# A causal convolution's taps read from the transposition's PSUM bank, over whole rows, and a norm with both heads' reciprocals ahead of both products

## The chip, the core and the metric

The kernel runs on one core of a Trainium2 chip. The core has a matrix engine (PE, TensorE), three engines for elementwise work (DVE or VectorE, ACT or ScalarE, POOL or GpSimd), and SP, which here only issues DMA transfers. SBUF is the large on-chip memory. PSUM is the small memory that PE writes its results to. The metric is the time of one execution on the device in microseconds, the median of several runs.

## The reference, cut to what matters

```python
# attention: B=8, H=8, S=576, D=64
scores = (1/sqrt(D)) * q @ k.T                     # per batch and head
cum = cumsum(maximum(s, 0.0))
scores = where(causal, -1e9, scores + minimum(-(cum_i - cum_j), 0.0))
attn = exp(scores - max)
attn = attn / (sum(attn) + 1e-09)
x = attn @ v                                       # (B, S, 512) with the heads side by side
# gated linear unit with a causal convolution of 5 taps over S, per channel
gate_pre[:, t] = sum over k of conv_w[k] * x[:, t - 4 + k]
gate = 1 / (1 + exp(-gate_pre))
out = (gate * (x @ w_val)) @ w_out
```

## The kernel before

The work is cut into 32 passes n = 4b + p: a batch b (8 of them) and a pair of heads p (4 pairs), which makes 128 of the 512 channels of x. A pass goes through these steps:

- `scores` and `exps`: PE computes the scores of both heads in three steps into two double banks `s`, ACT takes the exponential of each step (L583) and writes the tile `P`.
- `av`: PE multiplies P with V, one head after the other, each into a PSUM bank of its own. Column 64 of each of the five row blocks is the row sum.
- `norm`: DVE takes the reciprocal of the row sums (L599) and multiplies (L600). The result goes to `xn` in SBUF. It is called once for each head.
- `x_T`: PE transposes the 128 channels of the pass into a bank as 128 channels by 576 positions, in bf16.
- `x_evac`: DVE copies the bank (L611) into `xT` in SBUF, behind four columns of zeros.
- `tap`: five taps of the convolution. The row of 576 is done in two halves of 288. The first tap of a half writes the product of x and one weight per channel (L623 on ACT or L625 on DVE) into a PSUM bank `gs`. Each of the other four (L629, on DVE) reads xT shifted by one column, multiplies and adds the sum. Three of them write back to the bank and the last one writes the tile `gp` in SBUF. The table `ON_ACT` gives the first taps of 21 of the 32 passes to ACT.
- `tanh`: ACT turns gp into `th` (L633).
- `val` and `glu`: when all four passes of a batch are in xT, PE multiplies x with w_val (L653), in two halves for each pass, and DVE multiplies each half with the gate (L659).
- `outp`, `out_evac`, `store`: PE multiplies with w_out (L665), ACT copies to SBUF (L670), SP stores.

Eight PSUM banks exist. Four of them are the two double banks of the scores. The other four, named m0 to m3, are shared by all else: the transpositions of q and k (`qk_T`, copied by ACT at L533), the two heads of av, x, gs, val and out. Of gp there are two buffers, so that a tap that writes gp first waits for the tanh of the pass two before.

The order is not written by hand. Each step is a task with an engine, an assumed duration, the tasks it depends on, the buffers it takes and gives back, and a due time, which is the pass number plus an offset from the table `DUE`. The class `Plan` plays the tasks through once before the program is built: every engine takes the ready task with the earliest due time. The instructions are then emitted in that order, and each engine works through its own list strictly in that order. At run time an instruction waits for the instructions that it depends on, also on its own engine.

The weights of the convolution come transposed as `cwT` (L478). The scaled w_val is `wv` (L455). Both stand on DVE ahead of the first tap. On SP the load of w_val (L453) stands behind the loads of the first two batches of q and k.

Of the kernel before, what the change touches and what calls it, by code (L numbers as in the profile page):

```python
# [16 lines left out]
B, H, S, D = 8, 8, 576, 64  # L17
DM = 512
NKB = 5
# [184 lines left out]
def pcol(kb, qb):  # L204
    if kb == qb:
        return kb * 128
    if qb == 4:
# [13 lines left out]

DUE = dict(av=0.35, norm=0.78, xt=0.86, xe=-3.88, tap=1.56, dtap=0.01, tanh=0.36, cpe=-12.17, val=4.61,
           dval=0.23, out=9.61, dout=0.77, oute=-13.36, qt=-3.41, qe=-3.11, tt=-2.05, te=-14.54, s4=-1.53,
           vp=-12.15, cast=-20.65, lqk=-9.83, lv=17.78)

ON_PE = ()
PE_CHUNK = 2

ON_ACT = tuple(n for n in range(32) if n % 3)


class Plan:
# [115 lines left out]
def main_path(ctx, tc, q, k, v, s, moe_w_val, moe_conv_w, moe_w_out, out, okcnt):  # L350
# [5 lines left out]
    nc = tc.nc  # L356
# [125 lines left out]
    T = {}  # L482
# [110 lines left out]
                nc.tensor.matmul(ps[:, qb * 65:qb * 65 + 65], lhsT, Vps[b % 2][:, kb, 2 * p + hh, :],  # L593
                                 start=(kb == 0), stop=(kb == qb))

    def norm(n, hh):
        b, p = divmod(n, 4)
        pv = slot["av", n, hh].rearrange("t (g d) -> t g d", d=65)
        nc.vector.reciprocal(recs[:, n, hh], pv[:, :, 64])  # L599
        nc.vector.tensor_tensor(xns[b % 2][:, :, p * 128 + hh * 64:p * 128 + hh * 64 + 64], pv[:, :, 0:64],  # L600
                                recs[:, n, hh].unsqueeze(2).to_broadcast([128, NKB, 64]), ALU.mult)

    def x_T(n):
        b, p = divmod(n, 4)
        pt = slot["x", n] = bank(("x", n), [128, S], BF16)
        for i in (4, 0, 1, 2, 3):
            nc.tensor.transpose(pt[:, WIN[i]:WIN[i] + 128], xns[b % 2][:, i, p * 128:(p + 1) * 128], ident)  # L607

# [1 line left out]
        b, p = divmod(n, 4)  # L610
        nc.vector.tensor_copy(xTs[b % 2][:, p, 4:4 + S], slot["x", n])  # L611

    def tap(n, hf, m):

        b, c = divmod(n, 4)
        o = hf * 288
        xc = xTs[b % 2][:, c, o:o + 292]
        if m == 0:
            slot["gs", n, hf] = bank(("gs", n, hf), [128, 288])
            if hf == 0:  # L620
                slot["g", n] = work("gp", n, [128, S], FP32)
            if n in ON_ACT:
                nc.scalar.activation(out=slot["gs", n, hf], in_=xc[:, 4:292], func=AF.Copy, scale=cwT[:, c, 4:5])  # L623
            else:
                nc.vector.tensor_scalar(slot["gs", n, hf], xc[:, 4:292], cwT[:, c, 4:5], None, ALU.mult)  # L625
        else:
            gs = slot["gs", n, hf]
            dst = slot["g", n][:, o:o + 288] if m == 4 else gs
            nc.vector.scalar_tensor_tensor(dst, xc[:, m - 1:m + 287], cwT[:, c, m - 1:m], gs, ALU.mult, ALU.add)  # L629

    def tanh(n):
        th = slot["t", n] = work("th", n, [128, S], FP32)
# [42 lines left out]
    for b in range(B):  # L675
# [58 lines left out]
        for p in range(4):  # L734
            n = n0 + p
            es = []
            for i in range(3):
                take = [("s", ("s", n, i))] + ([("P", n)] if i == 0 else [])
                t = T["s", n, i] = add("PE", (0.56, 0.27, 0.27)[i], n + 0.3 * i, lambda n=n, i=i: scores(n, i),
                                       [T["qe", b, p], t_te, T.get(("s", n, i - 1)), T.get(("s", n - 1, 2))],  # L740
                                       take=take, mode="R")
                es.append(add("ACT", 0.905, n + 0.3 * i, lambda n=n, i=i: exps(n, i), [t],
                              give=[("s", ("s", n, i))]))
            ns = []
            for hh in range(2):
# [3 lines left out]
                ns.append(add("DVE", 0.62, n + DUE["norm"] + 0.1 * hh, lambda n=n, hh=hh: norm(n, hh),  # L749
                              [t, T.get(("xt", n - 8))], give=[("m", ("av", n, hh))]))  # L750
            T["norm", n] = ns[1]
            t = T["xt", n] = add("PE", 0.3, n + DUE["xt"], lambda n=n: x_T(n), ns, take=[("m", ("x", n))], mode="N")

            T["xe", n] = add("DVE", 0.37, n + DUE["xe"], lambda n=n: x_evac(n),
                             [t] + [T.get(("val", n0 - 8 + c, hf)) for c in range(4) for hf in range(2)]
                             + T.get(("conv", n - 8), []), give=[("m", ("x", n))])
            ths = []
            if PE_CONV(b, p):
                cs = []
                for hf in range(2):  # L760
                    t = add("PE", 1.85, n + DUE["cpe"], lambda n=n, hf=hf: conv_pe(n, hf), [T["xe", n], t_dg] + cs[-1:],
                            take=[("m", ("g", n, hf))], mode="N")
                    cs.append(t)
                    ths.append(add("ACT", 0.42, n + DUE["cpe"] + 0.2, lambda n=n, hf=hf: tanh_pe(n, hf), [t] + ths,
                                   take=[("th", n)] if hf == 0 else [], give=[("m", ("g", n, hf))]))
                T["conv", n] = cs
            else:
                ends = []
                for hf in range(2):
                    t = ends[0] if hf else None  # L770
                    for m in range(5):
                        take = [("gp", n)] if m + hf == 0 else []
                        if m == 0:
                            take = take + [("m", ("gs", n, hf))]
                        t = add("ACT" if m == 0 and n in ON_ACT else "DVE", 0.37, n + DUE["tap"] + (hf * 2.5 + m * 0.5) * DUE["dtap"],
                                lambda n=n, hf=hf, m=m: tap(n, hf, m), [T["xe", n], t_cw, t], take=take,
                                give=[("m", ("gs", n, hf))] if m == 4 else [])
                    ends.append(t)
                T["conv", n] = ends
# [102 lines left out]
```

## Time and profile before

| | |
|---|---|
| time, median of 3 runs | 270.92 us (270.29 to 271.18) |
| time of the profiled execution | 271.83 us |
| its span | 270.0 us |
| mean granted TensorE clock | 0.938 |
| taps on DVE (L625, L629) | 278 instructions, 143.8 us |
| first taps on ACT (L623) | 42 instructions, 21.1 us |
| norm on DVE, whole run (L599, L600) | 64 + 64 instructions, 12.0 + 31.5 us |
| copies of x on DVE (L611) | 32 instructions, 14.5 us |

The span runs from the first to the last instruction of the program. The rest of an execution's time lies around it. A row of the profile for a group of instructions gives the line, the engine, the operation, the tiles written and read, the shapes and the count, then the busy time and the mean duration in ns, and then the idle time of the engine just before these instructions with what ended it. A row of waits says who waited for whom, with the sum in us, the number of times and the longest one.

### The profile page before, as it was taken

The numbers are of one execution on the slowest core, as the hardware profiler recorded it, in microseconds if no ns is written. First come the engines' busy times: TensorE is split into PE (matmuls) and PEld (weight loads), VectorE is DVE, ScalarE is ACT, GpSimd is POOL, SyncE is SP. The second block draws the span as 40 slices with busy tenths as digits, with TensorE's granted clock in tenths as the row PEclk, the third lists the DMA queues.
The fourth block names the chain that finished last, engine by engine and source line by source line (L and its number), as shares of the span: only waits on it lengthen the run. The fifth ranks groups of instructions, "written<-read, shape, count | busy, mean of one in ns | idle before, by whom it ended". The sixth has DMA issues, their size and how long they took to land. (4 is left out here: it accounts for less than half of the span.)

```text
span 270.0 us, 6360 instructions
## 1 busy us (share of the span) xinstructions
PE 197.8 (73%) x2539; PEld 127.8 (47%) x2561; DVE 226.0 (84%) x524; ACT 194.9 (72%) x267; POOL 73.3 (27%) x73
## 2 busy tenths in 40 slices
PE   0788776766598679876849886887878776986660
PEld 0465642554456445553436553555445544543420
DVE  4453699899999898999987998999899999999920
ACT  2789788434888989878865787977987797684330
POOL 9204236457022810300930057042033000000000
PEclk9999965688889999999967999999999999999998
DMA  6999999989259970794421910752560120043133
GB/s 168 258 297 304 179 264 300 195 230 328 62 187 227 311 233 23 165 261 142 162 71 26 224 68 2 168 107 80 122 114 37 53 89 2 2 155 136 42 104 105
DMA packets 69232, 40.50 MB, mean 150 GB/s; under 512 B 47109, under 2 KB 63493, under 8 KB 69194
## 3 DMA queue, kind: packets, MB, share of 16 engines
q1 hardware_dynamic: 69194, 40.01, 56.7%
q8 instruction: 22, 0.36, 0.6%
q14 instruction: 16, 0.13, 0.2%
HBM read 30.57 MB, written 9.44 MB: 148 GB/s over the span
## 5 line engine op out<-in xcount | busy, mean ns | idle before, releaser
L583 ACT ACTIVATE P<-s 128x1024 bf16<-128x1024 f32 x96 | 95.1, 1027 | 14.4 <-PE s L580 9.5
L629 DVE SCALAR_TENSOR_TENSOR m<-xT,cwT,m 128x288 f32<-128x288 bf16 x192 | 99.6, 521 | 6.3 <-ACT m L623 1.6
L653 PE MATMUL m<-xT,wv 128*128 128x288 bf16 x256 | 43.6, 309 | 10.1 <-DVE gp L629 8.5
L538 PE MATMUL s<-QKT 64*128 64x128 bf16 (+4 forms) x576 | 41.4, 253 | 13.0 <-ACT P L583 10.6
L593 PE MATMUL m<-Vp,P 128*128 128x65 bf16 x960 | 40.8, 199 | 10.1 <-DVE gp L629 7.4
L500 POOL TENSOR_TENSOR Vp<-vst,w 128x650 bf16<-128x650 f32 x28 | 35.1, 1283 | 42.2 <-DMA vst<-in_v_dram 36.7
L665 PE MATMUL m<-wo,glu 128*128 128x512 bf16 x138 | 39.5, 384 | 9.5 <-DVE gp L629 7.3
L593 PEld LDWEIGHTS <-P 128*128 128x128 bf16 x960 | 36.4, 101 | 19.2 <-DVE gp L629 8.0
L538 PEld LDWEIGHTS <-QKT 64*128 64x128 bf16 x576 | 21.6, 99 | 34.0 <-issue 26.3
L533 ACT COPY QKT<-m 128x1024 bf16<-128x1024 bf16 x32 | 32.2, 1017 | 6.5 <-PE m L529 6.3
L653 PEld LDWEIGHTS <-wv 128*128 128x128 bf16 x256 | 24.6, 103 | 23.3 <-issue 13.6
L629 DVE SCALAR_TENSOR_TENSOR gp<-xT,cwT,m 128x288 f32<-128x288 bf16 x64 | 32.8, 514 | 2.1
L633 ACT ACTIVATE th<-gp 128x576 f32<-128x576 f32 x32 | 21.9, 684 | 15.9 <-DVE gp L629 15.6
L600 DVE TENSOR_TENSOR xn<-m,recs 128x320 bf16<-128x320 f32 x64 | 31.5, 492 | 2.2
L623 ACT ACTIVATE m<-xT,cwT 128x288 f32<-128x288 bf16 x42 | 21.1, 506 | 15.9 <-DVE glu L659 5.8
L670 ACT COPY ot<-m 128x512 f32<-128x512 f32 (+1 forms) x40 | 23.3, 584 | 11.9 <-PE m L665 9.4
L659 DVE SCALAR_TENSOR_TENSOR glu<-th,m 128x288 bf16<-128x288 f32 x64 | 26.7, 448 | 1.8 <-PE m L653 1.5
L665 PEld LDWEIGHTS <-glu 128*128 128x128 bf16 x160 | 14.4, 98 | 22.8 <-issue 7.5
L490 POOL CAST qb<-qkf 128x2048 bf16<-128x2048 f32 x7 | 13.3, 1894 | 37.1 <-issue 22.4
L529 PE MATMUL m<-ident,qb 128*128 128x128 bf16 x128 | 13.1, 227 | 12.0 <-DVE chalf L432 6.4
L607 PE MATMUL m<-ident,xn 128*128 128x128 bf16 x160 | 14.8, 225 | 6.4 <-DVE xn L600 5.1
L611 DVE COPY xT<-m 128x576 bf16<-128x576 bf16 x32 | 14.5, 452 | 4.4 <-PE m L607 4.3
(59 smaller groups left out, 160.2 us busy)
## 6 DMA issues: line engine op xcount, KB each, us to landing
out_dram<-ot SPq DMA_DIRECT2D x32, 256.0 KB, 2.1
qkf<-in_q_dram SPq DMA_DIRECT2D x7, 1024.0 KB, 5.9
qkf<-in_k_dram SPq DMA_DIRECT2D x7, 1024.0 KB, 7.9
vst<-in_v_dram SPq DMA_DIRECT2D x28, 256.0 KB, 5.0
vst<-in_v_dram SPq DMA_DIRECT2D x15, 128.0 KB, 4.3
first<-in_q_dram SPq DMA_DIRECT2D x4, 256.0 KB, 3.5
first<-in_k_dram SPq DMA_DIRECT2D x4, 256.0 KB, 3.6
tail<-in_q_dram SPq DMA_DIRECT2D x8, 128.0 KB, 8.8
```

The lines of the kernel that those rows point to most:

```text
L500: eng.tensor_tensor(Vps[b % 2][:, :, h], vst[:, :, h], w[:, :, b * 8 + 2 * p:b * 8 + 2 * p + 2].unsqueeze(3).to_broadcast([128, NKB, 2, 65 ...
L533: nc.scalar.copy(QKTs[b % 2][:, :, p, 0:512].rearrange("d w (x j) -> d w x j", j=4), slot["qt", b, p].rearrange("d w (j x) -> d w x j", j=4))
L538: nc.tensor.matmul(ps[:, hh, c0:c0 + nq], QKTs[b % 2][r, 1, p, k0:k0 + 128], QKTs[b % 2][r, 0, p, q0:q0 + nq], **kw)
L583: nc.scalar.activation(out=slot["Pt", n][:, :, step * 512:(step + 1) * 512], in_=slot["s", n, step], func=AF.Exp, scale=0.125)
L593: nc.tensor.matmul(ps[:, qb * 65:qb * 65 + 65], lhsT, Vps[b % 2][:, kb, 2 * p + hh, :], start=(kb == 0), stop=(kb == qb))
L600: nc.vector.tensor_tensor(xns[b % 2][:, :, p * 128 + hh * 64:p * 128 + hh * 64 + 64], pv[:, :, 0:64], recs[:, n, hh].unsqueeze(2).to_broad ...
L629: nc.vector.scalar_tensor_tensor(dst, xc[:, m - 1:m + 287], cwT[:, c, m - 1:m], gs, ALU.mult, ALU.add)
L633: nc.scalar.activation(out=th, in_=slot["g", n], func=AF.Tanh, scale=0.5)
L653: nc.tensor.matmul(ps, wv[:, dc, c * 128:(c + 1) * 128], xTs[b % 2][:, dc, 4 + o:4 + o + 288], start=(dc == 0), stop=(dc == 3))
L659: nc.vector.scalar_tensor_tensor(glus[b % 2][:, c, o], slot["t", n][:, o], 1.0, slot["v", n, hf], ALU.add, ALU.mult)
L665: nc.tensor.matmul(ps, glus[b % 2][:, c, WIN[i]:WIN[i] + 128], wo[:, c, :], start=(c == 0), stop=(c == 3))
L670: nc.scalar.copy(ot[r, :], slot["o", b, i][r, :])
```

## The change

Each pass loses the two banks gs. The taps read the bank of x itself, not the copy in SBUF, and run over the whole row in one piece. The sum is kept in gp in SBUF from the first tap on, which is a product alone, written with the newest weight over all 576 columns. The other four add x times an older weight, shifted to the right by `sh` = 4, 3, 2 and 1 columns, over the columns from sh on, so the zeros ahead of xT aren't needed by the taps. The bank of x is given back by the fifth tap and no longer by the copy. The copy stays, since val reads it. All first taps go to DVE. A norm is one task for both heads: two reciprocals and then two products. It starts when both heads' av are done, and gives both banks back at its end. The transposition of x also takes a gp buffer, in the plan. The table of due times is another one, which moves tasks on all engines.

```diff
-DUE = dict(av=0.35, norm=0.78, xt=0.86, xe=-3.88, tap=1.56, dtap=0.01, tanh=0.36, cpe=-12.17, val=4.61,
...
+DUE = dict(av=0.31, norm=0.64, xt=1.09, xe=0.37, tap=1.88, dtap=0.55, tanh=0.13, cpe=-12.44, val=4.58,
...
-ON_ACT = tuple(n for n in range(32) if n % 3)
+ON_ACT = ()
...
-    def norm(n, hh):
+    def norm(n):
         b, p = divmod(n, 4)
...
+        pvs = [slot["av", n, hh].rearrange("t (g d) -> t g d", d=65) for hh in range(2)]
+        for hh in range(2):
+            nc.vector.reciprocal(recs[:, n, hh], pvs[hh][:, :, 64])
+        for hh in range(2):
+            nc.vector.tensor_tensor(xns[b % 2][:, :, p * 128 + hh * 64:p * 128 + hh * 64 + 64], pvs[hh][:, :, 0:64],
+                                    recs[:, n, hh].unsqueeze(2).to_broadcast([128, NKB, 64]), ALU.mult)
...
-    def tap(n, hf, m):
+    def tap(n, m):
...
+        x, gp = slot["x", n], slot["g", n]
+        sh = (4 - (m - 1)) % 5 if m else 0
         if m == 0:
...
-                nc.vector.tensor_scalar(slot["gs", n, hf], xc[:, 4:292], cwT[:, c, 4:5], None, ALU.mult)
+                nc.vector.tensor_scalar(gp, x, cwT[:, c, 4:5], None, ALU.mult)
         else:
-            gs = slot["gs", n, hf]
-            dst = slot["g", n][:, o:o + 288] if m == 4 else gs
-            nc.vector.scalar_tensor_tensor(dst, xc[:, m - 1:m + 287], cwT[:, c, m - 1:m], gs, ALU.mult, ALU.add)
+            nc.vector.scalar_tensor_tensor(gp[:, sh:S], x[:, 0:S - sh], cwT[:, c, 4 - sh:5 - sh], gp[:, sh:S],
+                                           ALU.mult, ALU.add)
...
-                             + T.get(("conv", n - 8), []), give=[("m", ("x", n))])
+                             + T.get(("conv", n - 8), []), give=[("m", ("x", n))] if on_pe else [])
...
+                t = T["xe", n]
+                for m in range(5):
+                    act = m == 0 and n in ON_ACT
+                    t = add("ACT" if act else "DVE", 0.54 if act else 0.67, n + DUE["tap"] + m * DUE["dtap"],
+                            lambda n=n, m=m: tap(n, m), [t_cw, t], give=[("m", ("x", n))] if m == 4 else [])
```

How the order moves is seen at three places. In the rows the number right behind a name is the buffer (m0 to m3 are the four shared banks), and the number behind the underscore tells one use of it from another. In the kernel after the change the reciprocal stands at L600, the product at L602, the copy at L615, the first tap at L626 and the others at L628; the lines of before are those named above.

The first place is DVE in pass 21, in the second half of the run. Before, with the sum in the bank m3:

```order
L625 TENSOR_SCALAR m3_3005<-xT1_119,cwT_130 128x288
L629 SCALAR_TENSOR_TENSOR m3_3005<-xT1_119,cwT_130,m3_3005 128x288 x3
L629 SCALAR_TENSOR_TENSOR gp1_3006<-xT1_119,cwT_130,m3_3005 128x288
L599 RECIPROCAL recs_126<-m0_3008 128x5
L600 TENSOR_TENSOR xn1_117<-m0_3008,recs_126 128x5x64
L625 TENSOR_SCALAR m3_3064<-xT1_119,cwT_130 128x288
L629 SCALAR_TENSOR_TENSOR m3_3064<-xT1_119,cwT_130,m3_3064 128x288 x2
L611 COPY xT1_119<-m2_3073 128x576
L629 SCALAR_TENSOR_TENSOR m3_3064<-xT1_119,cwT_130,m3_3064 128x288
L629 SCALAR_TENSOR_TENSOR gp1_3006<-xT1_119,cwT_130,m3_3064 128x288
L599 RECIPROCAL recs_126<-m0_3082 128x5
L600 TENSOR_TENSOR xn1_117<-m0_3082,recs_126 128x5x64
```

Behind the first of these rows the sum of the first half is finished in gp1, then comes a norm of one head, and then the second half. After, with x in the bank m1 and the sum in gp1:

```order
L615 COPY xT1_119<-m1_2824 128x576
L626 TENSOR_SCALAR gp1_2825<-m1_2824,cwT_130 128x576
L628 SCALAR_TENSOR_TENSOR gp1_2825<-m1_2824,cwT_130,gp1_2825 128x572
L628 SCALAR_TENSOR_TENSOR gp1_2825<-m1_2824,cwT_130,gp1_2825 128x573
L600 RECIPROCAL recs_126<-m2_2833 128x5
L600 RECIPROCAL recs_126<-m3_2859 128x5
L602 TENSOR_TENSOR xn1_117<-m2_2833,recs_126 128x5x64
L602 TENSOR_TENSOR xn1_117<-m3_2859,recs_126 128x5x64
L628 SCALAR_TENSOR_TENSOR gp1_2825<-m1_2824,cwT_130,gp1_2825 128x574
L628 SCALAR_TENSOR_TENSOR gp1_2825<-m1_2824,cwT_130,gp1_2825 128x575
```

Before, the ten taps of the pass stand in two runs of five with a norm of one head between and one behind them, and the second run has the copy of the next pass in it. After, the copy is followed at once by the first tap of the same pass, five taps stand in the place of ten, and the norm of the next pass stands as four instructions between the third tap and the fourth.

The second place is ACT at about the same time, in passes 22 and 23. Before:

```order
L623 ACTIVATE m0_3160<-xT1_119,cwT_130 128x288
L583 ACTIVATE P0_3047<-s0_3128 128x2x512
L670 COPY ot0_3182<-m3_3152 128x512
L623 ACTIVATE m2_3197<-xT1_119,cwT_130 128x288
L533 COPY QKT1_113<-m1_3171 128x2x512
L558 ACTIVATE P40_100<-s0_3185 128x8x64
L583 ACTIVATE P1_3137<-s1_3136 128x2x512
L670 COPY ot1_3236<-m0_3213 64x512
L623 ACTIVATE m3_3254<-xT1_119,cwT_130 128x288
L623 ACTIVATE m0_3273<-xT1_119,cwT_130 128x288
L583 ACTIVATE P1_3137<-s0_3230 128x2x512
L583 ACTIVATE P1_3137<-s1_3277 128x2x512
```

Four of these twelve rows are first taps (L623). After, from the tanh of pass 21 to that of pass 22 and one row on:

```order
L633 ACTIVATE th3_2971<-gp1_2825 128x576
L583 ACTIVATE P0_2878<-s1_2966 128x2x512
L583 ACTIVATE P1_2976<-s0_2975 128x2x512
L533 COPY QKT0_112<-m3_2995 128x2x512
L583 ACTIVATE P1_2976<-s1_3005 128x2x512
L670 COPY ot0_3055<-m0_3012 128x512
L558 ACTIVATE P40_100<-s0_3029 128x8x64
L533 COPY QKT1_113<-m3_3045 128x2x512
L633 ACTIVATE th4_3077<-gp0_2916 128x576
L670 COPY ot1_3095<-m0_3065 64x512
```

The first taps between the exponentials, copies and tanhs are gone from ACT's list, and nothing stands in their place.

The third place is DVE at the first taps of the run. Before, from the third copy on:

```order
L611 COPY xT0_118<-m2_513 128x576
L599 RECIPROCAL recs_126<-m1_519 128x5
L600 TENSOR_TENSOR xn0_116<-m1_519,recs_126 128x5x64
L599 RECIPROCAL recs_126<-m3_536 128x5
L600 TENSOR_TENSOR xn0_116<-m3_536,recs_126 128x5x64
L611 COPY xT0_118<-m1_605 128x576
L455 TENSOR_SCALAR wv_127<-qkf2_175 128x2048
L478 COPY cwT_130<-m2_633 128x20
L625 TENSOR_SCALAR m1_640<-xT0_118,cwT_130 128x288
L629 SCALAR_TENSOR_TENSOR m1_640<-xT0_118,cwT_130,m1_640 128x288 x3
L629 SCALAR_TENSOR_TENSOR gp0_641<-xT0_118,cwT_130,m1_640 128x288
L625 TENSOR_SCALAR m0_673<-xT0_118,cwT_130 128x288
```

Here four norms and four copies stand ahead of wv, cwT and the first tap. After, from the scaling of wv on:

```order
L455 TENSOR_SCALAR wv_127<-qkf2_175 128x2048
L478 COPY cwT_130<-m2_557 128x20
L626 TENSOR_SCALAR gp0_351<-m0_350,cwT_130 128x576
L628 SCALAR_TENSOR_TENSOR gp0_351<-m0_350,cwT_130,gp0_351 128x572
L626 TENSOR_SCALAR gp1_441<-m3_440,cwT_130 128x576
L628 SCALAR_TENSOR_TENSOR gp0_351<-m0_350,cwT_130,gp0_351 128x573
L628 SCALAR_TENSOR_TENSOR gp1_441<-m3_440,cwT_130,gp1_441 128x572
L628 SCALAR_TENSOR_TENSOR gp0_351<-m0_350,cwT_130,gp0_351 128x574
L600 RECIPROCAL recs_126<-m1_515 128x5
L600 RECIPROCAL recs_126<-m2_609 128x5
L602 TENSOR_TENSOR xn0_116<-m1_515,recs_126 128x5x64
L602 TENSOR_TENSOR xn0_116<-m2_609,recs_126 128x5x64
```

Ahead of these rows stand three norms and two copies, so that wv, cwT and the first tap have moved ahead of one norm and two copies. The taps of passes 0 and 1 alternate, out of the banks m0 and m3, and the norm of the fourth pass stands between them.

More of the change, by code (lines that the diff above doesn't have):

```diff
@@ L605, in x_T @@
         pt = slot["x", n] = bank(("x", n), [128, S], BF16)
+        if not PE_CONV(b, p):
+            slot["g", n] = work("gp", n, [128, S], FP32)
         for i in (4, 0, 1, 2, 3):
@@ L748, in main_path @@
                                         give=[("P", n)] if hh else [], mode="N")
[L749 to L752, printed above, removed]
+            ns = [add("DVE", 1.1, n + DUE["norm"], lambda n=n: norm(n), [t, T.get(("xt", n - 8))],
+                      give=[("m", ("av", n, hh)) for hh in range(2)])]
+            T["norm", n] = ns[0]
+            on_pe = PE_CONV(b, p)
+            t = T["xt", n] = add("PE", 0.3, n + DUE["xt"], lambda n=n: x_T(n), ns,
+                                 take=[("m", ("x", n))] + ([] if on_pe else [("gp", n)]), mode="N")
             T["xe", n] = add("DVE", 0.37, n + DUE["xe"], lambda n=n: x_evac(n),
                              [t] + [T.get(("val", n0 - 8 + c, hf)) for c in range(4) for hf in range(2)]
[L756 removed]
+                             + T.get(("conv", n - 8), []), give=[("m", ("x", n))] if on_pe else [])
             ths = []
@@ L767, in main_path @@
             else:
[L768 to L779, printed above, removed]
+                t = T["xe", n]
[3 more added lines that the diff above has]
+                            lambda n=n, m=m: tap(n, m), [t_cw, t], give=[("m", ("x", n))] if m == 4 else [])
+                T["conv", n] = [t]
                 ths = [add("ACT", 0.59, n + DUE["tanh"], lambda n=n: tanh(n), [t], take=[("th", n)], give=[("gp", n)])]
```

15 lines of the change are left out of this document (3 added, 12 removed).

## The prediction

> **What bounds the kernel now.** I read the page first for the busy shares, then the span cut into three stretches, then what VectorE (DVE) waits for, and last the starts of neighbouring DVE instructions.
>
> ```profile
> PE 197.8 (73%) x2539; PEld 127.8 (47%) x2561; DVE 226.0 (84%) x524; ACT 194.9 (72%) x267; POOL 73.3 (27%) x73
> ...
> 0.00:33.70 33.70, 21.91 (x333) 16.24 (x334) 16.86 (x37) 24.66 (x33) 13.00 (x28) 1.00 0.96 241
> 33.70:258.40 224.70, 171.91 (x2189) 110.01 (x2211) 209.16 (x487) 167.35 (x231) 60.34 (x45) 0.93 0.53 138
> 258.40:270.00 11.60, 3.94 (x19) 1.57 (x16) 0.00 (x0) 2.92 (x5) 0.00 (x0) 0.89 0.32 110
> ```
>
> The cuts are the first tap (33.7 us) and the last glu product (258.4 us). In each row the length comes first, then PE, PEld, DVE, ACT and POOL. Between the cuts DVE is busy 209.16 of 224.70 us, so 15.5 us are left. Few of them are waits for another engine:
>
> ```profile
> DVE xT L611 <- PE m L607: 1.6, 2, 1.2
> DVE m L629 <- ACT m L623: 1.6, 3, 0.6
> DVE glu L659 <- PE m L653: 1.5, 4, 0.5
> DVE recs L599 <- PE m L593: 0.7, 2, 0.4
> ```
>
> These are 5.4 us; the rest is the hand-over from one DVE instruction to the next. So in this stretch the time is DVE's: its list of work, one after the other. Before it DVE is half idle (DMA share 0.96), behind it DVE does nothing. What DVE does there:
>
> ```profile
> L629 DVE SCALAR_TENSOR_TENSOR m<-xT,cwT,m 128x288 f32<-128x288 bf16 x192 | 99.6, 521 | 6.3 <-ACT m L623 1.6
> L629 DVE SCALAR_TENSOR_TENSOR gp<-xT,cwT,m 128x288 f32<-128x288 bf16 x64 | 32.8, 514 | 2.1
> L600 DVE TENSOR_TENSOR xn<-m,recs 128x320 bf16<-128x320 f32 x56 | 27.5, 492 | 1.9
> L659 DVE SCALAR_TENSOR_TENSOR glu<-th,m 128x288 bf16<-128x288 f32 x64 | 26.7, 448 | 1.8 <-PE m L653 1.5
> L611 DVE COPY xT<-m 128x576 bf16<-128x576 bf16 x28 | 12.6, 452 | 1.7 <-PE m L607 1.6
> L625 DVE TENSOR_SCALAR m<-xT,cwT 128x288 f32<-128x288 bf16 x22 | 11.4, 517 | 0.6
> L599 DVE RECIPROCAL recs<-m 128x5 f32<-128x5 f32 x56 | 10.4, 187 | 1.0 <-PE m L593 0.7
> ```
>
> The taps (L629 and L625, 278 instructions) are 143.8 us of it. What one instruction really takes of the list is the distance between starts:
>
> ```profile
> 149.92 0.18 DVE L599 RECIPROCAL recs<-m 128x5 f32<-128x5 f32 x1
> 150.14 0.49 DVE L600 TENSOR_TENSOR xn<-m,recs 128x320 bf16<-128x320 f32 x1
> 150.55 1.63 DVE L629 SCALAR_TENSOR_TENSOR m<-xT,cwT,m 128x288 f32<-128x288 bf16 x3
> 152.08 0.45 DVE L611 COPY xT<-m 128x576 bf16<-128x576 bf16 x1
> 152.45 0.50 DVE L629 SCALAR_TENSOR_TENSOR gp<-xT,cwT,m 128x288 f32<-128x288 bf16 x1
> 152.88 0.18 DVE L599 RECIPROCAL recs<-m 128x5 f32<-128x5 f32 x1
> ...
> 162.91 0.45 DVE L611 COPY xT<-m 128x576 bf16<-128x576 bf16 x1
> 163.47 0.52 DVE L625 TENSOR_SCALAR m<-xT,cwT 128x288 f32<-128x288 bf16 x1
> ...
> 173.64 1.17 DVE L659 SCALAR_TENSOR_TENSOR glu<-th,m 128x288 bf16<-128x288 f32 x3
> ```
>
> A tap whose result the next instruction reads takes (1.63 − 0.52)/2 = 0.555 us: its duration and 0.035 of hand-over. A tap with a stranger behind it takes 152.88 − 152.45 = 0.43: the stranger starts 0.09 before the tap ends. Likewise reciprocal 0.22 with its product behind it, product 0.41, copy 0.37 (0.56 where the next tap reads what it copied), glu (1.17 − 0.45)/2 = 0.36.
>
> In the order of before, 191 of the 278 taps stand ahead of an instruction that reads their result and 87 do not; 20 copies stand ahead of a reader, 8 do not. So the list is 191 × 0.555 + 87 × 0.43 = 143.4; 28 passes × 2 × 0.63 = 35.3 of norms; 20 × 0.56 + 8 × 0.37 = 14.2 of copies; 64 × 0.36 = 23.0 of glus; 2.5 for the scaling of wo and the check of the reciprocals: 218.4. With 5.4 of waits it is 223.8 of the 224.7 measured. The method misses 0.9 us, which I carry along.
>
> **Taps, part one: their number and length.** The ten half-row taps of a pass become five of 572 to 576 columns; all five are on DVE. No row shows this instruction. Its length follows from two others:
>
> ```profile
> L500 DVE TENSOR_TENSOR Vp<-vst,w 128x650 bf16<-128x650 f32 x4 | 3.3, 833 | 4.1 <-DMA vst<-in_v_dram 2.9 <-ACT w L445 1.2
> ...
> L811 DVE SCALAR_TENSOR_TENSOR ok<-recs,ok 128x320 f32<-128x320 f32 x1 | 0.5, 492 | 0.0
> ```
>
> 330 more columns cost 341 ns, 1.033 ns each. A tap of 288 columns takes 521 ns, so 576 take 0.521 + 288 × 0.00103 = 0.82 us. Ends: the glu row, which also reads PSUM and SBUF and writes SBUF, gives 0.448 + 0.298 = 0.75; two half taps without any saving give 1.04. I take 0.82, the same operation with the same per-partition factor. The first tap (a product alone) has as near relatives L625, 0.517 + 0.298 = 0.815, and the copy L611, 0.452 for the whole row, since that moves bf16 to bf16; its output is now f32 as L625's is, so 0.82 too.
>
> [...]
>
> **Part two: who stands behind a tap.** In the new order only 60 of 160 taps are followed by the next tap of their own chain; 100 have a stranger behind them. Taps: 60 × (0.82 + 0.035) + 100 × (0.82 − 0.09) = 51.3 + 73.0 = 124.3, against 143.4.
>
> **Norms and copies.** Two reciprocals stand together, and the first product needs only the first of them, so the pair hides in the 0.22 that one took: 0.22 + 2 × 0.41 = 1.04 per pass instead of 1.26. One pass more than before falls behind the first tap: 29 × 1.04 = 30.2. The first tap reads the PSUM bank, no longer the copy, so every copy takes 0.37: 30 × 0.37 = 11.1 (two more than before). Glus 23.0 and the 2.5 stay. New list: 124.3 + 30.2 + 11.1 + 23.0 + 2.5 = 191.1, which is 27.3 less.
>
> **Start and end of the stretch.** The first tap still needs the scaled wv and cwT ahead of it:
>
> ```profile
> 19.78 1.26 SPq L453 DMA_DIRECT2D qkf<-in_moe_w_val_dram  x1
> ...
> qkf<-in_moe_w_val_dram SPq DMA_DIRECT2D x1, 1024.0 KB, 11.1
> ...
> 31.93 1.65 DVE L455 TENSOR_SCALAR wv<-qkf 128x2048 bf16<-128x2048 f32 x1
> 33.50 0.16 DVE L478 COPY cwT<-m 128x20 f32<-128x20 f32 x1
> 33.77 0.52 DVE L625 TENSOR_SCALAR m<-xT,cwT 128x288 f32<-128x288 bf16 x1
> ```
>
> wv lands at 19.78 + 11.1 = 30.9. SP's order is the same up to there, and the row that made DVE late (the fourth copy) now stands behind, so the first tap comes at 30.9 + 1.84 = 32.7. The tail of 11.6 us keeps its work: tanh, val, glu, out, copy and store of the last pass.
>
> **ScalarE, POOL, SP.** ScalarE loses 42 first taps, and with them DVE's 1.6 us of waits for it:
>
> ```profile
> L623 ACT ACTIVATE m<-xT,cwT 128x288 f32<-128x288 bf16 x42 | 21.1, 506 | 15.9 <-DVE glu L659 5.8 <-DVE xT L611 4.7 <-DVE gp L629 2.6
> ```
>
> They are off the path (ACT is busy 167.35 of 224.70), so the 21.1 us are worth only those 1.6; I leave them in the waits, as new ones will take their place. POOL's casts and products and SP's loads move by a few places; no DVE wait names either, so I price this at nothing. Their cover is POOL's 164 idle us in the stretch.
>
> **New waits.** A bank of x is now held from its transposition through all five taps: 0.37 + 4 × 0.73 + 0.855 with a norm of 1.04 between, about 5.2 us. Before, it was 0.8 for x and two sums of 5 × 0.555, 6.4 us. The first head's bank is held some 0.5 longer. So the four banks carry about as much, in a shorter time. What DVE can now outrun is PE:
>
> ```profile
> 103.70 2.33 PE L653 MATMUL m<-xT,wv 128*128 128x288 bf16 x16
> ...
> 151.78 0.62 PE L593 MATMUL m<-Vp,P 128*128 128x65 bf16 x15 [0.17 <-ACT ot L670]
> ...
> PE m L653 <- DVE gp L629: 8.5, 10, 1.7
> PE m L593 <- DVE gp L629: 7.4, 10, 1.5
> PE m L665 <- DVE gp L629: 7.3, 8, 1.4
> ```
>
> A val takes 2.33/4 = 0.58 and a glu 0.36, so 64 glus in unbroken runs would wait 64 × 0.22 = 14 us. Many have taps between them; I take half, 7 us (ends 0 and 14).
>
> **Sum.** 32.7 + 191.1 + 0.9 + 5.4 + 11.6 = 241.7 of span. The profiled execution of before took 271.83 for a span of 270.0, so 243.5; the median of 270.92 is 0.9 below it, so 242.6; with 7 of new waits **249.5**.
>
> **Rivals.** (1) DVE waits for the pair of heads. A norm now starts only when both AV products are done; if PE makes the second one late each time, 29 × 0.62 = 18 us, 260.6. For it: a norm took its first bank while PE worked on the second. Against it: PE waits for banks that DVE's taps hold (the three rows, 23 us), so PE is the one that is ahead.
>
> (2) No overlap behind a tap. If a stranger waits until the tap is through, 100 taps cost 0.855 instead of 0.73: 12.5 us, 262. Against it stand the starts at 152.45 and 152.88. [...]
>
> (3) Shorter taps, 0.75 by the glu row: 160 × 0.07 = 11 us, 238.5.
>
> (4) Slower. With two passes' x open, two of four banks are taken and a pair of heads takes the rest; PE can then start the next pair only when DVE has ended a chain, and DVE waits for the whole pair, 2 × 0.62 = 1.24 us, in each of 32 passes: 242.6 + 39.7 = 282. It decides from (270.9 − 242.6)/32 = 0.88 us a pass. Against it: per pass the banks are held no longer than before.
>
> (5) The change doesn't do what it says: a long tap costs two short ones, 1.04. Then 160 × 0.22 = 35 us, 285. The slope speaks against it.
>
> **Chances.** Forecast (240 to 256) 0.61, (1) 0.16, (2) 0.05, (3) 0.10, (4) 0.06, (5) 0.02. The range 238 to 262 leaves out about 2 in 10. Slower by over 0.3% (what a measurement here can tell; the three runs spread by that) 0.07, within 0.3% 0.02, faster 0.91.
>
> **What would show it.** Taps of 0.82 us in 160 rows; start distances of 0.73 and 0.855; a norm in 1.04; the first tap near 32.7; no L623 kind of row on ACT; DVE's waits near 12 us, most of them of glu for PE's val. Wrong would be a tap far from 0.82, or waits of DVE for PE above 20 us, and then which instruction waits tells (1) from (4).

## The result and the profile after

The kernel after takes 244.8 us (median of four runs, 244.4 to 245.4) beside 271.05 us for the kernel before on the same chip. The ratio is 0.904, with a 95% interval from 0.901 to 0.907. The profiled execution took 244.44 us for a span of 242.7 us.

First the busy line of the page, then the span in three stretches (length, PE, PEld, DVE, ACT and POOL busy, clock, DMA share and GB/s). The cuts are again the first tap and the end of the last glu product:

```profile
PE 186.9 (77%) x2561; PEld 125.2 (52%) x2561; DVE 203.8 (84%) x406; ACT 175.5 (72%) x225; POOL 74.2 (31%) x73
...
0.00:33.30 33.30, 19.37 (x272) 13.69 (x273) 14.22 (x31) 22.49 (x29) 12.39 (x28) 1.00 0.94 238
33.30:230.40 197.10, 163.21 (x2270) 109.79 (x2270) 189.47 (x376) 150.11 (x191) 61.85 (x46) 0.98 0.61 158
230.40:242.70 12.30, 4.32 (x20) 1.76 (x18) 0.08 (x1) 2.92 (x5) 0.00 (x0) 0.80 0.34 114
```

The middle stretch went from 224.70 to 197.10 us, and that is the whole gain of 27.3 us in span: the start gave 0.4 more and the end took 0.7 back. DVE's share of the page is 84% as before, so this share alone says nothing of the gain. What the gain consists of is seen in DVE's groups and waits in the middle stretch:

```profile
L628 DVE SCALAR_TENSOR_TENSOR gp<-m,cwT,gp 128x574 f32<-128x574 bf16 (+3 forms) x128 | 102.1, 811 | 2.1
L626 DVE TENSOR_SCALAR gp<-m,cwT 128x576 f32<-128x576 bf16 x32 | 25.9, 809 | 0.7 <-ACT th L633 0.7
...
L602 DVE TENSOR_TENSOR xn<-m,recs 128x320 bf16<-128x320 f32 x58 | 25.6, 484 | 0.0
```

```profile
DVE xT L615 <- PE m L611: 2.0, 4, 0.9
...
DVE glu L659 <- PE m L653: 1.2, 2, 0.7
DVE recs L600 <- PE m L593: 0.8, 3, 0.3
DVE gp L626 <- ACT th L633: 0.7, 1, 0.7
```

These waits are 4.7 us (5.4 before). What is left, 197.1 − 4.7 = 192.4 us, is DVE's list, against 224.7 − 5.4 = 219.3 before. So 26.9 us of the gain are list and 0.7 are waits. The start distances, from DVE's timeline at three places:

```profile
34.19 0.81 DVE L628 SCALAR_TENSOR_TENSOR gp<-m,cwT,gp 128x572 f32<-128x572 bf16 x1
34.92 0.81 DVE L626 TENSOR_SCALAR gp<-m,cwT 128x576 f32<-128x576 bf16 x1
...
58.32 0.26 DVE L600 RECIPROCAL recs<-m 128x5 f32<-128x5 f32 x2
58.54 0.89 DVE L602 TENSOR_TENSOR xn<-m,recs 128x320 bf16<-128x320 f32 x2
59.35 1.66 DVE L628 SCALAR_TENSOR_TENSOR gp<-m,cwT,gp 128x573 f32<-128x573 bf16 x2
```

A tap with a stranger behind it takes 34.92 − 34.19 = 0.73 us of the list. Two taps of one chain last 1.66 us together, which is one distance and one duration: 1.66 − 0.81 = 0.85. A norm of two heads takes 59.35 − 58.32 = 1.03.

PE, for its part, hardly waits for DVE's taps any more. The three rows that stood at 8.5, 7.4 and 7.3 us in the prediction are now, in PE's waits over the whole span:

```profile
PE s L538 <- ACT P L583: 7.0, 13, 2.1
...
PE m L653 <- DVE gp L628: 2.4, 4, 0.9
PE m L593 <- DVE gp L628: 1.9, 2, 1.5
```

The third, of outp (L665) for a tap, is down to 0.2, so 23.2 us have become 4.5. A wait is put to whichever instruction came last, though, and part of this has moved to norms and glus: with all of DVE's instructions counted, the same three steps of PE waited 25.8 us before and wait 13.2 us now.

### The profile page after: what moved, and what is told of

It is laid out like the page before. It is cut to its first block, busy times and chain, and to the rows that moved or that the text cites. A ratio compares the mean times of both kernels' runs of the same rounds, so it can differ in the third digit from the quotient of the medians.

```text
span 242.7 us, 6220 instructions
## 1 busy us (share of the span) xinstructions
PE 186.9 (77%) x2561; PEld 125.2 (52%) x2561; DVE 203.8 (84%) x406; ACT 175.5 (72%) x225; POOL 74.2 (31%) x73
## 5 line engine op out<-in xcount | busy, mean ns | idle before, releaser
L583 ACT ACTIVATE P<-s 128x1024 bf16<-128x1024 f32 x96 | 94.9, 1031 | 17.6 <-PE s L580 12.2
L628 DVE SCALAR_TENSOR_TENSOR gp<-m,cwT,gp 128x574 f32<-128x574 bf16 (+3 forms) x128 | 102.1, 811 | 2.1
L538 PE MATMUL s<-QKT 64*128 64x128 bf16 (+4 forms) x576 | 39.9, 248 | 8.8 <-ACT P L583 7.0
L653 PE MATMUL m<-xT,wv 128*128 128x288 bf16 x256 | 39.1, 286 | 8.8 <-DVE glu L659 3.1
L500 POOL TENSOR_TENSOR Vp<-vst,w 128x650 bf16<-128x650 f32 x28 | 35.0, 1281 | 30.2 <-DMA vst<-in_v_dram 25.2
L665 PE MATMUL m<-wo,glu 128*128 128x512 bf16 x160 | 39.7, 379 | 5.1 <-DVE xn L602 3.7
L593 PE MATMUL m<-Vp,P 128*128 128x65 bf16 x960 | 38.9, 196 | 4.5 <-DVE gp L628 1.9
L593 PEld LDWEIGHTS <-P 128*128 128x128 bf16 x960 | 35.3, 99 | 11.1 <-issue 4.2
L533 ACT COPY QKT<-m 128x1024 bf16<-128x1024 bf16 x32 | 32.7, 1023 | 8.4 <-PE m L529 8.3
L653 PEld LDWEIGHTS <-wv 128*128 128x128 bf16 x256 | 23.2, 97 | 20.4 <-issue 12.4
L538 PEld LDWEIGHTS <-QKT 64*128 64x128 bf16 x576 | 20.6, 97 | 23.4 <-issue 14.2
L633 ACT ACTIVATE th<-gp 128x576 f32<-128x576 f32 x32 | 22.2, 696 | 13.5 <-DVE gp L628 13.3
L490 POOL CAST qb<-qkf 128x2048 bf16<-128x2048 f32 x7 | 14.2, 2030 | 55.4 <-issue 21.9
L602 DVE TENSOR_TENSOR xn<-m,recs 128x320 bf16<-128x320 f32 x64 | 28.2, 482 | 0.0
L626 DVE TENSOR_SCALAR gp<-m,cwT 128x576 f32<-128x576 bf16 x32 | 25.9, 809 | 0.7 <-ACT th L633 0.7
L665 PEld LDWEIGHTS <-glu 128*128 128x128 bf16 x160 | 14.5, 97 | 19.6 <-issue 4.4
L529 PE MATMUL m<-ident,qb 128*128 128x128 bf16 x128 | 13.3, 231 | 12.4 <-DVE chalf L432 6.1
L529 PEld LDWEIGHTS <-qb 128*128 128x128 bf16 x128 | 8.8, 102 | 18.5 <-issue 10.3
L615 DVE COPY xT<-m 128x576 bf16<-128x576 bf16 x32 | 14.4, 451 | 2.6 <-PE m L611 2.6
```

Source lines behind the costliest of these rows:

```text
L500: eng.tensor_tensor(Vps[b % 2][:, :, h], vst[:, :, h], w[:, :, b * 8 + 2 * p:b * 8 + 2 * p + 2].unsqueeze(3).to_broadcast([128, NKB, 2, 65 ...
L533: nc.scalar.copy(QKTs[b % 2][:, :, p, 0:512].rearrange("d w (x j) -> d w x j", j=4), slot["qt", b, p].rearrange("d w (j x) -> d w x j", j=4))
L538: nc.tensor.matmul(ps[:, hh, c0:c0 + nq], QKTs[b % 2][r, 1, p, k0:k0 + 128], QKTs[b % 2][r, 0, p, q0:q0 + nq], **kw)
L583: nc.scalar.activation(out=slot["Pt", n][:, :, step * 512:(step + 1) * 512], in_=slot["s", n, step], func=AF.Exp, scale=0.125)
L626: nc.vector.tensor_scalar(gp, x, cwT[:, c, 4:5], None, ALU.mult)
L628: nc.vector.scalar_tensor_tensor(gp[:, sh:S], x[:, 0:S - sh], cwT[:, c, 4 - sh:5 - sh], gp[:, sh:S], ALU.mult, ALU.add)
```

## The experiments

Two theories stand against each other at first. **L, the list**: DVE is the bound, and the time follows the sum of its start distances. **R, the rival**: another engine or the turnover of the banks sets the pace by now (the expectations below name freed banks, an emptier ACT and a higher granted clock), so that a part of what the change saves on DVE is already hidden, and giving it back would cost little. Each kernel is the kernel after with one edit or two, but for one that is the kernel before. A median of four runs is given for each, with its ratio to the kernel before in the same series (medians of before 272.0, 271.6 and 271.55 us). The differences in us to the kernel after are taken between medians of different series, in which the kernel before itself differs by up to 1 us (271.05 to 272.0), so a single microsecond of them says nothing.

### The taps in halves again

```diff
-                nc.vector.tensor_scalar(gp, x, cwT[:, c, 4:5], None, ALU.mult)
+                for lo, hi in ((0, 288), (288, S)):
+                    nc.vector.tensor_scalar(gp[:, lo:hi], x[:, lo:hi], cwT[:, c, 4:5], None, ALU.mult)
...
+            for lo, hi in ((sh, 288), (288, S)):
+                nc.vector.scalar_tensor_tensor(gp[:, lo:hi], x[:, lo - sh:hi - sh], cwT[:, c, 4 - sh:5 - sh],
+                                               gp[:, lo:hi], ALU.mult, ALU.add)
```

> The kernel after with each tap issued as two halves of 288 columns, in the same place of the same order, from the same bank; nothing else is changed. Theory L (the time is DVE's list: count times start distance): 320 instructions of about 0.52 us with a stranger behind each, 320 x 0.42 = 134.4 us instead of 122.7, so about 244.8 + 12 = 256.5 us. Rival R (the gain came from the freed banks, the emptier ACT and a higher granted clock): all of these are as in the kernel after, so 245 to 247 us.

Measured: 255.6 us, ratio 0.940 (0.936 to 0.944). That is 10.8 us above the kernel after, as L had it. From its DVE timeline:

```profile
121.12 1.77 DVE L630 SCALAR_TENSOR_TENSOR gp<-m,cwT,gp 128x284 f32<-128x284 bf16 x4
122.81 0.25 DVE L600 RECIPROCAL recs<-m 128x5 f32<-128x5 f32 x2
```

Four half taps fill 122.81 − 121.12 = 1.69 us, 0.42 each, so two halves take 0.85 where one whole tap takes 0.73 with a stranger behind it. A half has another half behind it that doesn't read its result, so this kernel has no hand-over at all and still loses: two instructions of half the columns take 0.12 us more of the list than one, and this is what whole rows save.

### One head's norm after the other

```diff
         for hh in range(2):
             nc.vector.reciprocal(recs[:, n, hh], pvs[hh][:, :, 64])
-        for hh in range(2):
             nc.vector.tensor_tensor(xns[b % 2][:, :, p * 128 + hh * 64:p * 128 + hh * 64 + 64], pvs[hh][:, :, 0:64],
```

> The kernel after with the norm issued as reciprocal, product, reciprocal, product, in the same place of the same order. L: the second reciprocal no longer hides behind the first, 0.22 us in each of the 29 norms behind the first tap, 6.4 us, so about 251 us. R, and anyone who holds that the norm's order is hidden: 245 us.

Measured: 249.5 us, ratio 0.917 (0.914 to 0.921), 4.7 us above the kernel after. Its DVE timeline shows one norm:

```profile
122.03 0.18 DVE L600 RECIPROCAL recs<-m 128x5 f32<-128x5 f32 x1
122.25 0.49 DVE L601 TENSOR_TENSOR xn<-m,recs 128x320 bf16<-128x320 f32 x1
122.66 0.18 DVE L600 RECIPROCAL recs<-m 128x5 f32<-128x5 f32 x1
122.87 0.49 DVE L601 TENSOR_TENSOR xn<-m,recs 128x320 bf16<-128x320 f32 x1
123.28 0.81 DVE L627 SCALAR_TENSOR_TENSOR gp<-m,cwT,gp 128x574 f32<-128x574 bf16 x1
```

It takes 123.28 − 122.03 = 1.25 us instead of 1.03. Times 29 passes that is 6.4 us, and the span of the profiled run grew by 6.6 (249.3), the median by 4.7. The order of four neighbouring instructions is paid for nearly in full, as L has it.

### The kernel before, with all its first taps on DVE

```diff
-ON_ACT = tuple(n for n in range(32) if n % 3)
+ON_ACT = ()
```

> The kernel before with its 42 first taps of ScalarE given to VectorE; the plan then orders anew. L: 236 x 0.555 + 84 x 0.43 = 167.1 us of taps instead of 143.4, less 1.6 us of waits for ACT, so about 271 + 22 = 293 us. R: ACT gets 21 us emptier, so the time falls or stays, 265 to 272 us.

The plan orders the instructions anew for this. Measured: 296.4 us, ratio 1.088 (1.083 to 1.094): 24 us more than the kernel before for 42 half taps, 0.58 each. So the kernel before was bound by DVE's list too, and the change took 42 instructions on top of its own list and still won.

### Half of the output product left out

PE's own work could still be the bound behind DVE's. Here outp adds up two of the four channel blocks, and its sum ends at the second.

```diff
-        for c in range(4):
+        for c in range(2):
```

> The kernel after with half of the output product left out (it sums two of the four channel blocks), in the same order: PE has 80 matmuls, some 20 us, less to do. L: VectorE's list is the same, so only its 4 us of waits for PE and a microsecond or two of the tail can go: 239 to 244 us. If PE sets the pace of the kernel after as much as VectorE does: 225 to 235 us.

Measured: 243.65 us, ratio 0.897 (0.893 to 0.902), 1.2 us below the kernel after, about what the end of the run saves where DVE has nothing left to do (its stretch behind the last glu is 11.2 us long instead of 12.3). The middle stretch is no shorter than the 197.10 us of the kernel after:

```profile
32.80:230.50 197.70, 154.54 (x2201) 105.55 (x2201) 189.44 (x376) 150.30 (x191) 61.59 (x46) 0.96 0.59 158
```

The row of L665 is 23.7 us instead of 39.7, and PE is busy for 176.0 us of the run instead of 186.9. In the middle stretch this brings nothing: L holds, and R falls as far as PE goes.

### The old table of due times

All code of the change, with the `DUE` of before.

> The kernel after with the whole table of due times of before. 104 taps have a reader of their result behind them instead of 60, 44 x 0.125 = 5.5 us: 250.5 us if the table is worth only that; above 253 us if it also keeps VectorE from waiting for PE, as taps_in_a_row (8 us instead of 3.2) suggests; 245 us if the table is worth nothing.

Measured: 264.2 us, ratio 0.973 (0.967 to 0.978). Only 7 of the 26 us are left. The stretches of this kernel (the cuts are its own first tap and last glu), its DVE waits in the middle one, and its DVE timeline at one place:

```profile
31.05:245.70 214.65, 169.96 (x2239) 113.08 (x2239) 193.36 (x370) 149.34 (x187) 60.67 (x46) 0.94 0.54 142
245.70:262.00 16.30, 7.61 (x37) 3.12 (x34) 0.26 (x2) 5.26 (x9) 0.00 (x0) 0.90 0.39 134
```

```profile
DVE xT L615 <- PE m L611: 15.2, 22, 1.9
DVE glu L659 <- PE m L653: 1.3, 3, 0.5
DVE recs L600 <- PE m L593: 0.8, 3, 0.4
```

```profile
154.11 0.89 DVE L602 TENSOR_TENSOR xn<-m,recs 128x320 bf16<-128x320 f32 x2
155.55 0.46 DVE L615 COPY xT<-m 128x576 bf16<-128x576 bf16 x1 [0.55 <-PE m L611]
155.92 0.81 DVE L626 TENSOR_SCALAR gp<-m,cwT 128x576 f32<-128x576 bf16 x1
```

With `xe=-3.88` the copy of a pass is due far ahead of everything, so it stands right behind its own norm: 19 of 32 copies do so here, 2 in the kernel after. Between the two lies a transposition by PE, which starts only when the norm is done, and DVE stands still for it (0.55 us here). Against the kernel after, the waits are 17.3 instead of 4.7 us (+12.6), the list is 214.65 − 17.3 = 197.35 instead of 192.4 (+5.0, as 104 instead of 60 taps have a reader behind them), the end is 4.0 longer and the start 2.25 shorter: +19.3, as measured. The new table is thus worth 19 us together with the new code. The old code with the new table wasn't tried.

### Taps of a chain in a row

```diff
-... tap=1.88, dtap=0.55, ...
+... tap=1.88, dtap=0.01, ...
```

> The kernel after with the spacing of a pass's taps in the table of due times set back from 0.55 to 0.01, so that the plan puts more taps of one chain behind each other: 86 taps have a reader of their result behind them instead of 60. L: 26 x 0.125 = 3.2 us more, about 248 us. Rival (2) of the prediction (a stranger waits as long as a reader): 245 us.

Measured: 253.0 us, ratio 0.934 (0.929 to 0.938): 8 us more, where 86 instead of 60 taps ahead of a reader make 26 × 0.12 = 3.1. The waits in its middle stretch make about as much again:

```profile
DVE xT L615 <- PE m L611: 4.9, 7, 1.1
DVE recs L600 <- PE m L593: 2.0, 4, 1.2
DVE glu L659 <- PE m L653: 1.1, 2, 0.5
```

They are 8.0 instead of 4.7, and 3.1 + 3.3 is 6.4 of the 6.5 us by which the span of the profiled run grew (249.2). The spacing of a chain's taps does two things: a stranger behind a tap saves the hand-over (0.73 instead of 0.85 us in the kernel after), and the other work that stands between gives PE time for the next product (waits of 4.7 instead of 8.0 us).

### All taps from the copy in SBUF

The order stays, and so does the hold on the bank. Only the place that the taps read changes.

```diff
-                nc.vector.tensor_scalar(gp, x, cwT[:, c, 4:5], None, ALU.mult)
+                nc.vector.tensor_scalar(gp, xTs[b % 2][:, c, 4:4 + S], cwT[:, c, 4:5], None, ALU.mult)
...
-            nc.vector.scalar_tensor_tensor(gp[:, sh:S], x[:, 0:S - sh], cwT[:, c, 4 - sh:5 - sh], gp[:, sh:S],
+            nc.vector.scalar_tensor_tensor(gp, xTs[b % 2][:, c, m - 1:m - 1 + S], cwT[:, c, 4 - sh:5 - sh], gp,
```

> The kernel after with all five taps reading the copy of x in SBUF (576 columns each) instead of the PSUM bank; the order and the time at which the bank is given back are unchanged. L with equal tap lengths: the first tap now waits for the copy ahead of it, 28 x 0.19 = 5.3 us, so about 250 us. L with a faster first tap (0.51 us as the product over 576 columns at the program's start, L433): 32 x 0.30 = 9.6 us less, about 240.5 us. [...] R: no change, 245 us.

Measured: 281.7 us (four runs, 278.4 to 283.9), ratio 1.040 (1.033 to 1.047). This is the largest miss of the study: 37 us above the kernel after, for a change of nothing but the memory that is read. Its DVE groups, then its timeline of DVE and of POOL at one place:

```profile
L628 DVE SCALAR_TENSOR_TENSOR gp<-xT,cwT,gp 128x576 f32<-128x576 bf16 x128 | 134.6, 1064 | 2.1
L602 DVE TENSOR_TENSOR xn<-m,recs 128x320 bf16<-128x320 f32 x64 | 28.2, 482 | 0.0
```

```profile
104.82 10.18 DVE L628 SCALAR_TENSOR_TENSOR gp<-xT,cwT,gp 128x576 f32<-128x576 bf16 x6
...
117.10 1.67 DVE L628 SCALAR_TENSOR_TENSOR gp<-xT,cwT,gp 128x576 f32<-128x576 bf16 x2
```

```profile
105.48 1.90 POOL L490 CAST qb<-qkf 128x2048 bf16<-128x2048 f32 x1 [21.87 <-PE m L529]
107.35 7.04 POOL L500 TENSOR_TENSOR Vp<-vst,w 128x650 bf16<-128x650 f32 x4
114.34 2.42 POOL L490 CAST kb<-qkf 128x2048 bf16<-128x2048 f32 x1
```

Six taps take 10.18 us, 1.70 each, while POOL works, and two take 1.67 us, 0.84 each with their hand-over, once POOL has stopped at 116.8. POOL's V products suffer as well: 1.76 us each here (7.04/4) and 1281 ns on average in the kernel after. The norm's product, which reads only its small factors from SBUF, stays at 482 ns. So a new theory: a tap whose tensors are all in SBUF and POOL's casts and products hold each other up.

### The same with POOL's later work left out

To the edit above is added that POOL's casts and V products run for the first two batches only (`if b < 2`), so that the later batches compute with old data.

> sbuf_source with POOL's casts and products of V left out for the batches 2 to 7 (the tiles keep the data of the first two batches), so that POOL is idle for most of the run; all five taps still read the copy in SBUF. If it is POOL's reading of SBUF that stretches the taps: they take 0.81 us and the first one 0.51, and the time falls from 282 to 238 to 247 us. If two operands in SBUF are slow by themselves: the taps stay near 1.06 us on average and the time stays above 270 us.

Measured: 244.6 us, ratio 0.902 (0.897 to 0.908), 37 us less than with POOL's work. The DVE group:

```profile
L628 DVE SCALAR_TENSOR_TENSOR gp<-xT,cwT,gp 128x576 f32<-128x576 bf16 x128 | 106.2, 843 | 2.1
L626 DVE TENSOR_SCALAR gp<-xT,cwT 128x576 f32<-128x576 bf16 x32 | 16.6, 519 | 2.0
```

The two groups of taps together fall from 134.6 + 20.7 to 122.8 us, 32.5 of the 34.6 by which the profiled span fell (276.6 to 242.0). That POOL's work is what stretched them is shown. The mean of 843 still holds some of it; from 100 to 230 us, where POOL does nothing, the row is

```profile
L628 DVE SCALAR_TENSOR_TENSOR gp<-xT,cwT,gp 128x576 f32<-128x576 bf16 x83 | 67.3, 815 | 1.7
```

The two-tensor taps of the kernel after, with one tensor in PSUM, are left alone: 811 ns on average over the run and 811 ns from 190 to 230 us, where POOL does nothing. The first tap, with its one tensor in SBUF, is not, as the next kernel shows. Whether it is POOL's reading of SBUF, as the expectation above has it, or another part of POOL's work was not shown.

### Only the first tap from SBUF

> The kernel after with only the first tap reading the copy of x in SBUF; the order is the same. In sbuf_source the first tap took 0.51 us, or more while POOL worked (mean 0.65), and stood 0.11 to 0.19 us behind its copy. L: 28 x 0.19 = 5.3 us more and 32 x 0.16 = 5.1 (at most 9.6) us less, 240.5 to 245 us, and the other four taps stay at 0.81 us, since they have one operand in SBUF beside the bank. If instead a source in SBUF is what slows a tap beside POOL, whatever the other operands: slower than 250 us.

Measured: 247.1 us, ratio 0.907 (0.902 to 0.913). That is between the two expectations, and the interval overlaps with that of the kernel after (0.901 to 0.907), so nothing is gained. The first tap has one tensor only, and without POOL it takes 519 ns from SBUF (above). In this kernel its mean doesn't get there:

```profile
L628 DVE SCALAR_TENSOR_TENSOR gp<-m,cwT,gp 128x574 f32<-128x574 bf16 (+3 forms) x128 | 102.1, 810 | 2.1
L626 DVE TENSOR_SCALAR gp<-xT,cwT 128x576 f32<-128x576 bf16 x32 | 24.1, 752 | 2.2 <-ACT th L633 0.3
```

The mean hides two kinds. In DVE's timeline 22 of the 32 take 0.50 to 0.52 us, and ten, each of them beside work of POOL, take 0.82 to 1.57:

```profile
144.43 0.52 DVE L626 TENSOR_SCALAR gp<-xT,cwT 128x576 f32<-128x576 bf16 x1
149.69 2.73 POOL L500 TENSOR_TENSOR Vp<-vst,w 128x650 bf16<-128x650 f32 x2
149.72 1.57 DVE L626 TENSOR_SCALAR gp<-xT,cwT 128x576 f32<-128x576 bf16 x1
```

So a source in SBUF slows this one-tensor tap beside POOL, as in the kernel with all taps from SBUF, and here the mean is 752 and not 646 as there (20.7 us over 32). 752 instead of 809 ns over 32 instructions are 1.8 us, and a tap that reads the copy must wait for the copy's end (0.56 instead of 0.37 in the rows of before). That costs more than it gains: added up from the timeline, the copies take 15.1 us of the list in the middle stretch instead of 11.1.

### First taps given away

ACT and POOL have idle time (busy 150.11 and 61.85 of the 197.10 us in the kernel after), so a shorter list was tried. In one kernel ACT takes the first tap of every third pass, in the other POOL that of every second, both from the copy in SBUF and with an order planned anew (assumed durations of 0.7 us for ACT, 0.8 for POOL and 0.73 for DVE).

```diff
-ON_ACT = ()
+ON_ACT = tuple(n for n in range(32) if n % 3 == 1)
...
+            xs = xTs[b % 2][:, c, 4:4 + S]
...
+                nc.scalar.activation(out=gp, in_=xs, func=AF.Copy, scale=cwT[:, c, 4:5])
+            elif n in ON_POOL:
+                nc.gpsimd.tensor_scalar(gp, xs, cwT[:, c, 4:5], None, ALU.mult)
```

> The kernel after with the first tap of 11 of the 32 passes on ScalarE, which reads the copy of x in SBUF (so that two engines don't read one bank); the plan orders anew. L: 49 x 0.845 + 100 x 0.72 = 113.4 us of taps on VectorE instead of 122.7, so about 235.5 us if ScalarE, busy 150 of 197 us, is in time; if it is late by half a microsecond in each of the 11 passes, 241 us. R (the emptier ACT is a source of the gain): 245 us or more.

> The kernel after with the first tap of every second pass on POOL, which reads the copy of x in SBUF; the plan orders anew. L: 41 x 0.845 + 103 x 0.72 = 108.8 us of taps on VectorE instead of 122.7, so about 231 us if POOL is in time. POOL's list waits for loads of v for up to 12 us at a time; if taps stand behind such a wait, VectorE waits with them and the time is 240 to 255 us.

Measured: 248.9 us with ACT, ratio 0.918 (0.914 to 0.922), and 258.4 us with POOL, ratio 0.953 (0.947 to 0.959). Neither helps. With POOL its late taps are the greater part of the reason: of the 30.3 us that DVE waits in the middle stretch, 17.6 stand in this row:

```profile
DVE gp L632 <- POOL gp L628: 17.6, 11, 7.3
```

With ACT the list did become shorter: the middle stretch has 199.96 us, and DVE's waits in it are

```profile
DVE xT L616 <- PE m L612: 6.3, 7, 2.4
DVE recs L601 <- PE m L594: 5.6, 10, 1.1
DVE glu L663 <- PE m L657: 1.8, 3, 1.0
DVE gp L632 <- ACT gp L626: 1.2, 1, 1.2
```

14.9 us, which leaves 185.1 for the list, 7.3 less than in the kernel after. The waits took 10.2. Three of the four rows are waits for PE, so PE's load was tried as the cause: the same kernel with half of the output product left out.

> act_third with the same half of the output product left out. VectorE's list is 9.3 us shorter there than in the kernel after, and its waits for PE were 14 us instead of 4. If PE is what took the gain: 231 to 239 us, clearly below less_pe. If the waits come from the order or from ACT and not from PE's load: 243 to 249 us, not below less_pe.

Measured: 244.7 us, ratio 0.902 (0.897 to 0.907), beside 243.65 us for the kernel after with the same half left out. The same four waits still are 13.3 us. Leaving out that half took 4.2 us off this kernel and 1.2 off the kernel after, so PE's load is at most a part of the cause. In the first of the two kernels, PE's waits in the middle stretch begin with

```profile
PE s L539 <- ACT P L584: 10.2, 18, 2.4
```

and this wait for the exponentials ahead of the scores is 5.4 us, 10 times, in the kernel after. So the first taps that stand ahead of exponentials on ACT are a suspect. That wasn't tested, and the cause stays open.

## Why the prediction was right, and where it was off

The sign and the range held. 249.5 us was 4.7 too high. By its steps:

- **What bounds the kernel**: right, and shown in one direction. Giving back a part of DVE's list costs about what the part measures (halves +10.8, norm +4.7, 42 half taps +24 on the kernel before), and 16 us of PE's work are worth 1.2. In the other direction it is not shown: with a list of 185.1 us (first taps on ACT), 181.0 (on POOL) and 190.9 (taps from SBUF without POOL's later work) no kernel was faster than the kernel after by more than a fraction of a microsecond.
- **The tap**: 0.82 predicted, 0.81 measured, distances 0.73 and 0.85 for 0.73 and 0.855. Rivals (2), (3) and (5) fall by these rows. A source in PSUM shows no price in the four taps with two tensors: 0.81 us from PSUM, and 0.815 from SBUF where POOL does nothing. The first tap does pay for it, 0.81 us against 0.52. The prediction set the copy's row of 0.452 us aside because the copy moves bf16 to bf16; no run shows that this is the reason, and the product with its f32 output took 0.52 us once it read SBUF. Taking all taps from the copy in SBUF cost 37 us here, through POOL.
- **Norm**: 1.04 predicted, 1.03 measured. Rival (1), that DVE waits for the pair of heads, stands at 0.8 us in three places, not at 18.
- **The list**: 191.1 + 0.9 = 192.0 predicted, 192.4 measured, and so close in part by luck. The count of 20 copies of before ahead of a reader is wrong. By DVE's timeline 22 of the 28 copies have the next start 0.36 to 0.38 us behind their own, even where a tap follows (152.08 and 152.45 in the prediction's rows), so that tap did not need the copied columns; only the copies at 162.91 and 240.36 have 0.56. Added up from the timeline, the copies of before took 11.2 us and not 14.2, the norms 37.0 and not 35.3, the glus 24.7 and not 23.0. After, they took 11.1, 30.0 and 25.0. So the copies gained next to nothing where 3.1 us were forecast, and the norms 7.0 where 5.1 were.
- **Start**: 33.3 instead of 32.7. wv was ready earlier than predicted, at 33.12 − 1.61 = 31.5, and then DVE waited 1.6 us for PE's transposition of the weights, ahead of cwT (L478). The prediction had counted the load alone.
- **End**: 12.3 instead of 11.6; of this 0.4 is PE's own work (4.32 instead of 3.94 us, at a granted clock of 0.80 instead of 0.89).
- **Waits**: 5.4 + 7 predicted, 4.7 measured. This is the term that was mis-sized, and more than the whole miss. The step said that DVE would outrun PE's val in half of the glus. glu waited 1.2 us in two places, less than before (1.5). A val still takes longer than a glu (four vals in a row take 2.12 us of PE from 99.03 on, 0.53 each, against 0.36), but the new order doesn't put glus in long runs (45 of the 64 stand alone or in pairs), and PE, whose waits for taps went from 23.2 to 4.5 us in those three rows, mostly had the vals done (that these two belong together is argued, not shown). Rival (4) falls here too: PE's waits for DVE shrank, and DVE's for PE stayed as they were (4.0 us in the rows of xT, glu and recs, 3.8 before).
- **From span to median**: the median of before lay 0.9 us below its profiled execution, and I carried that over. The median of after lies 0.4 above its own, 1.3 to the other side.

The sum of the differences: +0.6 +0.4 −7.7 +0.7 makes −6.0 in span, and +1.3 makes −4.7.

One thing the prediction got right without having priced it: it took the order as given, counted the taps with a reader behind them (60; under the old table there are 104, worth 5 us) and carried the old 5.4 us of waits along. The old table shows that this could not be taken for granted, and that it held was luck. With the same list to within 5 us, another order has 17.3 us of waits. The row that warns of it stood in the order, not in the profile: a copy right behind the norm whose transposition it must wait for.

## What to carry to other kernels

Where one engine's list is the bound, add up start distances, not durations, and count who stands behind whom: with whole-row instructions and strangers between the links of a chain counted so, the list came out at 192.0 us and was measured at 192.4, in part by luck. A shorter list brought nothing here where the waits grew with it, so it seems worth its length only with an order that keeps the other engine's product between two dependent instructions of the list, so look for each place where an instruction stands right behind the one that feeds it through another engine. And before moving an operand from PSUM to SBUF, look at which other engine works at that time: for the four two-tensor taps SBUF was no slower by itself here (0.815 us, 0.81 from PSUM), and with all five taps from SBUF the kernel lost 37 us through POOL.

## What the runs showed of the hardware that was not expected

- A 576-column scalar_tensor_tensor with both tensors in SBUF took 0.815 us while POOL did nothing and 1.70 us on average in a row of six beside POOL's casts and products, and POOL's four products took 7.04 us there and 5.00 us in the kernel after. With one tensor in PSUM the taps took 811 ns with and without POOL's work.
- The one-tensor product of the first tap took 0.52 us from SBUF where POOL did nothing, up to 1.57 us from SBUF beside POOL's work, and 0.81 us from PSUM in both cases.
